# Block-sparse attention into a SoLU layer on one core: the first batch's mask rows in two parts, and four reorderings towards the end of the plan

## The chip, the core and the metric

The kernel runs on one core of a Trainium2 chip. The core has five engines that run side by side and wait for each other by semaphores: TensorE (PE; matmuls and transposes, its weight loads shown apart as PEld), VectorE (DVE), ScalarE (ACT), GpSimd (POOL) and SyncE (SP, which here only issues DMAs). Each engine executes its own instructions in the order in which the program issues them. The metric is the device time of one execution in microseconds (us); less is better.

## The reference

Four batches of eight heads attend over 768 positions with a mask of 32-wide blocks; the result, put together over heads, goes through a layer whose activation is h times softmax(h), a normalisation and a second matmul.

```python
scores = scale * np.matmul(q, k.transpose(0, 1, 3, 2))          # B=4, H=8, S=768, D=64
mask = np.abs(blk_i - blk_j) <= 1                               # blocks of 32
mask |= (blk_i == 0) | (blk_j == 0) | (blk_i == n_blocks - 1) | (blk_j == n_blocks - 1)
...                                                             # and 3 sampled blocks per block row
attn = softmax(np.where(mask, scores, -1e9))
x = np.matmul(attn, v).transpose(0, 2, 1, 3).reshape(B * S, H * D)     # 3072 x 512

h = x @ w_in                                                    # 512 x 1024
solu = h * softmax(h)
ln = (solu - mean(solu)) / np.sqrt(var(solu) + 1e-06) * g_ln
out = ln @ w_out                                                # 1024 x 512
```

## The kernel before

**The attention.** Heads go in pairs (pr = 0 to 3). Queries and keys stand transposed in QT and KT, two of each, used by batches in turn. Partitions 0 to 63 hold the 64 elements of a head; partitions 64 to 87 (`D:KR`) hold mask rows: in KT a selector of the key's block, in QT the mask values of the query for each block. One matmul over 88 partitions thus gives scores with the mask already added (`scores`, L407 to L421). The mask rows are the same for all heads, so those of QT are made once for pair 0 (from `m_ps`, by ScalarE) and copied to the other pairs by `mask_rows` (L663 to L665), which reads `row_q`, the rows of head 0.

The 768 positions of a head are 6 chunks of 128. A pass takes 2 chunks of queries (QW = 256 positions), so a batch takes 3 passes and the kernel 12. A pass has 12 slots: 4 pairs times 3 units, each unit being 2 key chunks. In a slot TensorE makes scores for two slots ahead, ScalarE takes the exponential (`exps`, L423), and TensorE multiplies by the values (`outs`, L431); at the end of a pair VectorE divides by the sums (`normalise`, L451). Score buffers are two, buffers for exponentials three (each holds one pair), and the output of a pair has one PSUM buffer of each of two kinds in the first pass and one afterwards.

**The layer.** x of a pass is transposed by DMA (`x_turn`), except that the first pass and the last chunk of the last pass use TensorE (`x_first`, `x_last`). For each half of a pass: `h_mms` (eight matmuls on TensorE), `e_exp` (exponential with its sum, ScalarE), `solu` (VectorE), `ln_turn` (transposition by DMA), `stats` and `rstd` (VectorE, the root on GpSimd), `o_mms` (eight matmuls with weights whose mean was taken out, `w_cen_sb`), `scaled` and `store`. The layer of one pass runs inside the slots of the next. What is left of pass 10 and pass 11 comes behind the last slot in a list written out by hand (L945 to L983), where the transposition is done by TensorE (`ln_mm`, `ln_out`), the very last output is made in two column halves (`o_half`, `scale_half`), and a flag is worked out that says whether any sum was out of range (`check_r`, `check_e`, `check_sum`, `check_bad`, `check_out`). After everything all engines load the flag, and if it is set the whole is computed again by a slow general path; with these inputs it is not.

**The order.** `at(when, fn, ...)` puts a call on a plan; `emit` sorts the plan by its time in slots and issues it. So a number in `at` is a place in the queue of each engine that the call uses, not a time in microseconds: slot s is `s`, and 144 (`end`) is behind the last. Calls not under `at` are issued at once, before the plan. DMAs for loads, transpositions and most stores go through SP's queue, in the same order.

**Loading the first batch.** Only the first two query chunks of each pair are loaded and transposed at first (`load`, `cast`, `turn_mm`, `turn_out`), which suffices for pass 0; chunks 2 to 5 follow during pass 0 (`turn` at 8.9, 10.9, 14.95 and 16.95). Keys of pair 1 to 3 are transposed with their selector rows and copied out in two parts (`k_out`, L369). VectorE's mask copies of QT[0] stand among these: pair 1 before the plan (L685), pair 2 at 2.0 and pair 3 at 2.9 (L709, L710), each over all 768 positions of two heads, 24 partitions x 1536 elements. GpSimd casts loaded data to bf16 in the same stretch.

**Later batches.** GpSimd casts q and k into `nat`, one DMA per pair transposes both (`turn_dma`), and `shift` (L383) copies the two heads from `pd` into KT or QT on GpSimd, two instructions for each. The last pair's q is shifted in two parts (L806): its first two chunks just before k, and the rest later.

Of the kernel before, what the change touches and what calls it, by code (L numbers as in the profile page):

```python
# [7 lines left out]
FP32 = mybir.dt.float32  # L8
# [200 lines left out]
def kernel(  # L209
# [11 lines left out]
    nc = tc.nc  # L221

    B, H, S, D = q.shape
# [11 lines left out]
    KF = d_ff // 128  # L235
# [6 lines left out]
    PC = 2  # L242
    QW = PC * TQ
    NPB = NCH // PC
    NPASS = B * NPB
    NP = H // 2
# [27 lines left out]
    KT = [fix.tile([128, H * NCH, TQ], BF16, name=f"KT{i}") for i in range(2)]  # L274
    QT = [fix.tile([128, H * NCH, TQ], BF16, name=f"QT{i}") for i in range(2)]
# [14 lines left out]
    def at(when, fn, *args):  # L290
        plan.append((when, len(plan), fn, args))
# [282 lines left out]
    with tc.manual_schedule():  # L574
# [4 lines left out]
                          in_=bass.AP(tensor=_t32, offset=0, ap=[[2 * NR, NB], [1, 2 * NR]]))  # L579
# [59 lines left out]
        for pr in range(1, NP):  # L639
            nc.scalar.activation(  # L640
                out=natural(0, pr, "k")[:, :, :, D:KR].rearrange("p c h r -> p (c h) r"),
                in_=zer[:, 0:NB].rearrange("p (o r) -> p o r", o=1).broadcast_to(
                    [128, NCH * 2, NB]),
# [6 lines left out]
        sel_f = selT.rearrange("p c t -> p (c t)")  # L650
        for i, x0, x1 in ((0, 0, QW), (1, QW, S)):
            nc.tensor.matmul(m_ps[0:KR, i, 0 : x1 - x0], mask_l, sel_f[:, x0:x1],
                             start=True, stop=True)

        def rows(t, h0, h1):
            return t[D:KR].rearrange("p (h c) t -> p h (c t)", c=NCH)[:, h0:h1]

        def spread(x, n):
            return x.rearrange("p (o c) -> p o c", o=1).broadcast_to([NB, n, x.shape[-1]])

        row_q = QT[0][D:KR, 0:NCH, :].rearrange("p c t -> p (c t)")

        def mask_rows(eng, t, h0):  # L663
            eng.tensor_copy(out=rows(t, h0, h0 + 2),
                            in_=spread(sel_f if t in KT else row_q, 2))  # L665

        def selector(pr):
            for base, sg in ((0, 1), (BLK - 1, -1)):
# [11 lines left out]
        for h0, n, i, x0, x1 in ((0, 2, 0, 0, QW), (0, 1, 1, QW, S), (1, 1, 1, QW, S)):  # L680
            nc.scalar.copy(out=rows(QT[0], h0, h0 + n)[:, :, x0:x1],
                           in_=spread(m_ps[D:KR, i, 0 : x1 - x0], n))
        turn_out(0, 0, "q", DVE2, 0, 2)
        turn_out(0, 0, "k", DVE2, 2, NCH)
        mask_rows(nc.vector, QT[0], 2)  # L685
        cast(nc.gpsimd, 0, 1, "k")
        cast(nc.gpsimd, 0, 1, "q", 0, 2)
        scores(0, 2)
# [9 lines left out]
        def turn(when, b, pr, key, pool, c0=0, c1=NCH, engs=DVE2, later=0.02):  # L698
            at(when, turn_mm, b, pr, key, pool, c0, c1)
            at(when + later, turn_out, b, pr, key, engs, c0, c1)  # L700
# [5 lines left out]
        for pr in range(NP):  # L706
            at(0.1, load, nc.sync, q, 0, pr, "q", 2, NCH)

        for pr, w0, w1, w2 in ((2, 1.85, 2.85, 2.0), (3, 4.85, 5.85, 2.9)):  # L709
            at(w2, mask_rows, nc.vector, QT[0], 2 * pr)  # L710
            if pr == 3:
                selector(pr)
            cast(nc.gpsimd, 0, pr, "k")
            cast(nc.gpsimd, 0, pr, "q", 0, 2)
            at(w0, turn_mm, 0, pr, "k", p_h, 0, 2)
            at(w0 + 0.02, k_out, pr, 0, 2)
            turn(w0 + 0.01, 0, pr, "q", p_o, 0, 2)
            at(w1, turn_mm, 0, pr, "k", p_h, 2, NCH)
            at(w1 + 0.03, k_out, pr, 2, NCH)
# [50 lines left out]
        for s in range(n_units):  # L770
            ps, b, j, pr, u = unit(s)
# [25 lines left out]
        for b in range(1, B):  # L797
            loads, casts, turns, shifts, v_loads, v_casts = first if b == 1 else then
            t0 = SLOTS * NPB * (b - 1)
            for (key, pr), t_l, t_c in zip(kq + vs, loads + v_loads, casts + v_casts):  # L800
                at(t0 + t_l, load, nc.sync, srcs[key], b, pr, key)
                at(t0 + t_c, cast, nc.gpsimd, b, pr, key)
            for pr, t_t in enumerate(turns):
                at(t0 + t_t, turn_dma, b, pr)

            at(t0 + shifts[6] - 0.05, shift, b, NP - 1, "q", 0, PC)  # L806
            for (key, pr), t_s in zip(kq, shifts):
                at(t0 + t_s, shift, b, pr, key, PC if (key, pr) == ("q", NP - 1) else 0)


        def layer(ps, i, hs, es, os):
# [14 lines left out]
        LP = NPASS - 1  # L826
# [17 lines left out]
        for i, t0 in ((0, b0), (1, b0 + 4)):  # L844
            for when, n0, n1 in ((3.9, 0, 2), (4.85, 2, 5), (5.86, 5, 8)):
                at(t0 + when, h_mms, ps, i, n0, n1)

            e_at = (6.5, 7.0, 7.05) if i == 0 else (6.85, 6.86, 6.87)
            for when, fn in zip(e_at, (e_exp, solu, ln_turn)):
                at(t0 + when, fn, ps, i)  # L850
        at(b0 + 8.2, stats, ps, 0)
# [2 lines left out]
        def x_last():  # L854
            tp = p_op.tile([128, 1024], BF16, tag="op", name="x_tp")[:, 0 : PC * 128]
            for i in range(PC):
                nc.tensor.matmul(tp[:, i * 128 : (i + 1) * 128],
                                 xb_of[LP][:, KD - 1, i, :], ident,
                                 is_transpose=True, start=(i == 0), stop=(i == PC - 1))
            nc.vector.tensor_copy(  # L860
                out=xT_of[LP][:, (KD - 1) * PC : KD * PC, :],
                in_=tp.rearrange("p (i t) -> p i t", t=128))

# [22 lines left out]

        o2 = {}

        def o_half(half, pool, tag, c0=0, c1=KF):
            if c0:  # L890
                pass
            elif pool is p_sco:
                o2[half] = p_sco.tile([128, 2, HF], FP32, tag=tag, name="oe1a")[:, 0, 0:256]
            else:
                o2[half] = pool.tile([128, d_model], FP32, tag=tag, name="oe1b")[:, 0:256]
            for c in range(c0, c1):
                nc.tensor.matmul(o2[half], lnT_of[LP, 1][:, c, :],
                                 w_cen_sb[:, c, half * 256 : (half + 1) * 256],
                                 start=(c == 0), stop=(c == KF - 1), skip_group_check=True)
# [31 lines left out]
            nc.vector.tensor_scalar(out=bad, in0=n_ok[:, 0:1], scalar1=float(n_r + n_e),  # L931
                                    scalar2=None, op0=ALU.is_lt)

        bad_ps = []

        def check_bad():
            bad_ps.append(p_h.tile([1, 1], FP32, tag="h", name="bad_ps"))
            nc.tensor.matmul(bad_ps[0], bad, ones_c, start=True, stop=True)

        def check_out():  # L940
            nc.vector.tensor_copy(out=bad_i, in_=bad_ps[0])

        end = SLOTS * NPASS
        A, V = nc.scalar, nc.vector
        for n, (fn, *args) in enumerate((  # L945
            (h_end, 0, 2, KD),
            (e_exp, LP, 0),
            (o_mms, LP - 1, 0, 5, 8),
            (scaled, LP - 1, 0, A),
            (store, LP - 1, 0),  # L950
            (stats, LP - 1, 1),
            (rstd, LP - 1, 1),
            (check_r, n_r - 2 * PC, n_r),
            (h_end, 1, 0, KD),
            (solu, LP, 0),
            (stats, LP, 0),
            (e_exp, LP, 1),
            (o_mms, LP - 1, 1, 0, 3, tile_in(p_op, "op", "o_10")),
            (ln_mm, 0),
            (ln_out, 0, A),  # L960
            (o_mms, LP - 1, 1, 3, 8),
            (solu, LP, 1),
            (rstd, LP, 0),
            (stats, LP, 1),
            (o_mms, LP, 0, 0, 2, tile_in(p_sco, "sco", "oe0")),
            (ln_mm, 1),
            (ln_out, 1, A),
            (rstd, LP, 1),
            (check_e,),
            (check_sum,),  # L970
            (o_mms, LP, 0, 2, 8),
            (scaled, LP - 1, 1, A),
            (store, LP - 1, 1),
            (scaled, LP, 0, A),
            (store, LP, 0),
            (o_half, 0, p_sco, "sco"),
            (o_half, 1, p_op, "op", 0, 5),
            (check_bad,),
            (o_half, 1, p_op, "op", 5, KF),
            (scale_half, 0, V, nc.sync),  # L980
            (check_out,),
            (scale_half, 1, A, nc.scalar),
        )):  # L983
            at(end + 0.01 * n, fn, *args)
# [3 lines left out]
        at(end - 1.12, h_end, 0, 0, 2, (1,))  # L988
        at(end - 1.0, x_last)
        at(end - 1.9, check_r, 0, n_r - 2 * PC)  # L990
        at(end - 1.05, o_mms, LP - 1, 0, 0, 5)
        emit()

    work.close()
# [32 lines left out]
```

## Time and profile before

| what | value |
|---|---|
| time, median of 3 executions (lowest, highest) | 210.65 us (210.59, 210.71) |
| the profiled execution | 210.66 us |
| its span in the profile | 208.9 us |
| mean granted TensorE clock | 0.991 |
| engine totals of the page | shown in the prediction |
| DMA moved | 42.02 MB, mean 201 GB/s |

The span runs from the first instruction to the end of the last thing seen; what lies between it and the time is outside the profile. In rows of the timeline the columns are start and duration in us, engine, line of the kernel, operation, output <- inputs, shape, count, and in brackets how long the engine was idle before and for whom it waited; a row can stand for several like instructions in a run. The rows that begin with a stretch A:B give its length, then busy time (and count) of PE, PEld, DVE, ACT and POOL, the granted clock, the DMA share and GB/s. In rows of groups, total busy us and mean ns of one stand behind the bar. Durations of matmuls overlap, since they are pipelined: four matmuls that are shown as 0.60 us let the next one start after 0.44.

### The profile page before, as it was taken

To read this page: it belongs to the slowest core of one execution; us is meant where nothing else is said; L and a number is where in the kernel's file an instruction comes from. 1 tells how busy PE (TensorE), PEld (TensorE's weight loads), DVE (VectorE), ACT (ScalarE), POOL (GpSimd) and SP (SyncE) were. 2 spreads that over 40 slices of the span, in tenths; PEclk is the share of its full clock that TensorE was granted. 3 is DMA by queue.
4 is the path that set the end of the run, shared out by engine and by line. 5 is a ranking of instruction groups with operands and counts; after the bars stand their busy time and mean duration, and the time that the engine had idled before them with its cause. 6 is when DMAs were issued, how large, how long until landed. Compare 5 with 4: busy or idle time off the path is not lost.

```text
span 208.9 us, 5591 instructions
## 1 busy us (share of the span) xinstructions
PE 198.0 (95%) x2204; PEld 137.9 (66%) x2238; DVE 140.3 (67%) x329; ACT 174.6 (84%) x208; POOL 109.1 (52%) x161
## 2 busy tenths in 40 slices
PE   7989999999999999999999999999999999999980
PEld 2669867676676676676666677667667667665450
DVE  5885888987656656666656656656655755768970
ACT  6898989889889889889889889888988988875750
POOL 7989698688686384377196366197450011011120
PEclk9999999999999999999999999999999999999996
DMA  5999999899999899896999899997924915635331
GB/s 159 345 364 220 369 376 275 190 199 307 154 288 277 192 252 264 201 202 169 191 323 198 195 289 236 196 284 90 250 81 89 112 54 81 163 69 84 100 123 37
DMA packets 73906, 42.02 MB, mean 201 GB/s; under 512 B 55828, under 2 KB 69396, under 8 KB 73876
## 3 DMA queue, kind: packets, MB, share of 16 engines
q1 hardware_dynamic: 72932, 40.06, 80.4%
q0 software_dynamic: 528, 1.05, 2.7%
q10 hardware_dynamic: 416, 0.52, 0.8%
q8 instruction: 18, 0.29, 0.6%
q14 instruction: 12, 0.10, 0.2%
HBM read 23.07 MB, written 6.29 MB: 141 GB/s over the span
## 4 chain that ended last, share of the span: by engine, by line
PE 81%; DMA 9%; issue 2%; POOL 2%; ACT 1%; DVE 1%; SPq 1%; POOLq 0%
PE sco L416 28%; PE o L547 17%; PE op L444 16%; PE h L487 16%; DMA st_q<-in_q_dram 3%; DMA w_out_f<-in_moe_w_out_dram 3%; DMA st_k<-in_k_dram 3%; PE he L869 1%; PE oe L547 1%; PE mean_ps L750 1%; POOL VA L327 1%; SPq L318 1%; DVE solu L508 1%; POOL nat L327 1%; ACT e L496 1%
## 5 line engine op out<-in xcount | busy, mean ns | idle before, releaser
L427 ACT ACTIVATE exs<-sco 128x1024 bf16<-128x1024 f32 x144 | 140.6, 1024 | 8.7 <-PE sco L416 6.3
L416 PE MATMUL sco<-QT,KT 88*128 88x256 bf16 x576 | 86.6, 272 | 0.8 <-ACT exs L427 0.5
L416 PEld LDWEIGHTS <-KT 88*128 88x128 bf16 x576 | 54.1, 97 | 32.4 <-issue 5.7
L444 PE MATMUL op<-VA,exs 128*128 128x65 bf16 x1152 | 51.8, 194 | 0.5
L444 PEld LDWEIGHTS <-exs 128*128 128x128 bf16 x1152 | 48.5, 97 | 3.7 <-DVE xb L458 0.3
L487 PE MATMUL h<-w_in_sb,xT 128*128 128x512 bf16 x153 | 48.6, 378 | 0.6
L547 PE MATMUL o<-w_cen_sb,lnT 128*128 128x512 bf16 x166 | 43.2, 379 | 0.5
L540 POOL TENSOR_TENSOR rstd<-vpe,mhalf 128x1 f32<-128x1 f32 x24 | 13.2, 550 | 47.8 <-DVE vpe L538 41.3
L457 DVE RECIPROCAL recip_all<-op 128x4 f32<-128x4 f32 x48 | 8.7, 182 | 41.5 <-PE op L444 41.3
L496 ACT ACTIVATE e<-h 128x1024 bf16<-128x1024 f32 x22 | 22.5, 1024 | 12.3 <-PE h L487 10.8
L522 DVE BATCH_NORM_STATS2 stats<-solu 128x6 f32<-128x512 bf16 x48 | 30.6, 679 | 0.0
L327 POOL COPY KT<-pd 64x768 bf16<-64x768 bf16 x24 | 20.1, 838 | 17.4 <-DMA pd<-nat 15.8
L508 DVE TENSOR_TENSOR solu<-h,e 128x1024 bf16<-128x1024 f32 x22 | 26.7, 1215 | 1.4 <-ACT e L496 1.3
L327 POOL COPY QT<-pd 64x768 bf16<-64x768 bf16 (+2 forms) x30 | 20.8, 694 | 10.8 <-DMA pd<-nat 9.5
L547 PEld LDWEIGHTS <-lnT 128*128 128x128 bf16 x176 | 15.9, 97 | 13.8 <-DMA lnT<-solu 0.2
L558 DVE TENSOR_SCALAR ot<-o,rstd 128x512 f32<-128x512 f32 x20 | 15.0, 750 | 10.8 <-issue 6.9
L458 DVE TENSOR_TENSOR xb<-op,recip_all 128x256 bf16<-128x256 f32 x48 | 20.4, 424 | 1.7
L487 PEld LDWEIGHTS <-xT 128*128 128x128 bf16 x176 | 16.2, 98 | 4.2 <-DMA xT<-xb 0.5
L327 POOL CAST nat<-st_q 128x768 bf16<-128x768 f32 (+2 forms) x19 | 14.0, 736 | 7.8 <-DMA st_q<-in_q_dram 7.7
L327 POOL CAST nat<-st_k 128x768 bf16<-128x768 f32 x15 | 12.7, 850 | 3.3 <-DMA st_k<-in_k_dram 3.0
L327 POOL CAST VA<-st_v 128x768 bf16<-128x768 f32 x16 | 13.4, 842 | 1.9 <-DMA st_v<-in_v_dram 1.3
L740 POOL TENSOR_SCALAR w_out_sb<-w_out_f,g_ln_sb 128x512 bf16<-128x512 f32 x8 | 5.7, 724 | 2.1 <-DMA w_out_f<-in_moe_w_out_dram 2.1
(89 smaller groups left out, 114.7 us busy)
## 6 DMA issues: line engine op xcount, KB each, us to landing
st_v<-in_v_dram SPq DMA_DIRECT2D x16, 384.0 KB, 5.2
out_dram<-ot SPq DMA_DIRECT2D x23, 256.0 KB, 2.8
st_k<-in_k_dram SPq DMA_DIRECT2D x15, 384.0 KB, 5.4
st_q<-in_q_dram SPq DMA_DIRECT2D x12, 384.0 KB, 6.9
w_out_f<-in_moe_w_out_dram SPq DMA_DIRECT2D x4, 512.0 KB, 7.5
st_q<-in_q_dram SPq DMA_DIRECT2D x4, 256.0 KB, 6.9
w_in_sb<-in_moe_w_in_dram POOLq DMA_DIRECT2D x1, 1024.0 KB, 11.5
st_q<-in_q_dram SPq DMA_DIRECT2D x4, 128.0 KB, 4.7
```

What stands on the lines that cost most here:

```text
L327: eng.tensor_copy(out=o, in_=i)
L416: nc.tensor.matmul(sco[:, hh, kk * QW : (kk + 1) * QW], KT[b % 2][0:KR, h * NCH + 2 * u + kk, :], QT[b % 2][0:KR, h * NCH + PC * j : h * N ...
L427: nc.scalar.activation(out=exs_of[ps, pr][:, u].rearrange("p a b c -> p (a b c)"), in_=sco_of.pop(s).rearrange("p a b -> p (a b)"), func=A ...
L444: nc.tensor.matmul(op[:, hh, ic, :], exs[:, u, hh, kk, ic * TQ : (ic + 1) * TQ], VA[b % 2][:, 2 * pr + hh, 2 * u + kk, :], start=(u == 0 a ...
L458: nc.vector.tensor_tensor(out=xb_of[ps][:, pr].rearrange("p c (h d) -> p h c d", h=2), in0=op[:, :, :, 0:D], in1=recip.broadcast_to([TQ, 2 ...
L487: nc.tensor.matmul(h_of[ps, i][:, half, :], xT_of[ps][:, c * PC + i, :], w_in_sb[:, c, half * HF : (half + 1) * HF], start=(c == 0), stop= ...
L496: nc.scalar.activation(out=o, in_=h, func=ACT.Exp, scale=1.0, accum_out=esum_all[:, t : t + 1])
L508: nc.vector.tensor_mul(out=so, in0=h, in1=e)
L522: nc.vector.bn_stats(out=stat_of[ps, i][:, half, :], in_=so[:, half, :])
L540: nc.gpsimd.tensor_tensor(out=rstd_of[ps, i], in0=vpe, in1=mhalf, op=ALU.pow)
L547: nc.tensor.matmul(ops_of[ps, i], lnT_of[ps, i][:, c, :], w_cen_sb[:, c, :], start=(c == 0), stop=(c == KF - 1), skip_group_check=True)
L558: nc.vector.tensor_scalar(out=o, in0=i_, scalar1=r, scalar2=None, op0=ALU.mult)
```

## The change

It has five parts.

- `mask_rows` gets a range of positions. QT[0]'s mask rows of pairs 1, 2 and 3 are copied for the first 256 positions at first (pair 1 before the plan, pair 2 at 2.0, pair 3 at 0.87 instead of 2.9), and for the other 512 positions at 5.9, 7.9 and 8.99.
- The last pair's k of later batches is shifted in two parts like its q: first the first two chunks of k and of q, then the rest of k, and later the rest of q.
- The exponential e of the first half of pass 10's layer comes at 7.01 of the last pass instead of 6.5, which is behind that slot's exponential of scores instead of ahead of it.
- The copy in `x_last` goes to ScalarE, and of the five o matmuls ahead of it two are issued behind its transposes.
- At the end, the sum and the matmul and copy for the flag come behind `scale_half` of the first half instead of among the last matmuls, and `o_half` is in one piece.

```diff
-        def mask_rows(eng, t, h0):
-            eng.tensor_copy(out=rows(t, h0, h0 + 2),
-                            in_=spread(sel_f if t in KT else row_q, 2))
+        def mask_rows(eng, t, h0, x0=0, x1=S):
+            eng.tensor_copy(out=rows(t, h0, h0 + 2)[:, :, x0:x1],
+                            in_=spread((sel_f if t in KT else row_q)[:, x0:x1], 2))
...
-        mask_rows(nc.vector, QT[0], 2)
+        mask_rows(nc.vector, QT[0], 2, 0, QW)
...
-        for pr, w0, w1, w2 in ((2, 1.85, 2.85, 2.0), (3, 4.85, 5.85, 2.9)):
-            at(w2, mask_rows, nc.vector, QT[0], 2 * pr)
+        for pr, when in ((1, 5.9), (2, 7.9), (3, 8.99)):
+            at(when, mask_rows, nc.vector, QT[0], 2 * pr, QW, S)
+        for pr, w0, w1, w2 in ((2, 1.85, 2.85, 2.0), (3, 4.85, 5.85, 0.87)):
+            at(w2, mask_rows, nc.vector, QT[0], 2 * pr, 0, QW)
...
-            at(t0 + shifts[6] - 0.05, shift, b, NP - 1, "q", 0, PC)
             for (key, pr), t_s in zip(kq, shifts):
-                at(t0 + t_s, shift, b, pr, key, PC if (key, pr) == ("q", NP - 1) else 0)
+                if pr == NP - 1:
+                    at(t0 + shifts[6] - 0.1, shift, b, pr, key, 0, PC)
+                at(t0 + t_s, shift, b, pr, key, PC if pr == NP - 1 else 0)
...
-            e_at = (6.5, 7.0, 7.05) if i == 0 else (6.85, 6.86, 6.87)
+            e_at = (7.01, 7.02, 7.05) if i == 0 else (6.85, 6.86, 6.87)
...
-            nc.vector.tensor_copy(
+            nc.scalar.copy(
                 out=xT_of[LP][:, (KD - 1) * PC : KD * PC, :],
...
         def check_bad():
-            bad_ps.append(p_h.tile([1, 1], FP32, tag="h", name="bad_ps"))
-            nc.tensor.matmul(bad_ps[0], bad, ones_c, start=True, stop=True)
-
-        def check_out():
-            nc.vector.tensor_copy(out=bad_i, in_=bad_ps[0])
+            bad_ps = p_h.tile([1, 1], FP32, tag="h", name="bad_ps")
+            nc.tensor.matmul(bad_ps, bad, ones_c, start=True, stop=True)
+            nc.vector.tensor_copy(out=bad_i, in_=bad_ps)
...
             (check_e,),
-            (check_sum,),
...
             (o_half, 0, p_sco, "sco"),
-            (o_half, 1, p_op, "op", 0, 5),
+            (o_half, 1, p_op, "op"),
+            (scale_half, 0, V, nc.sync),
+            (check_sum,),
             (check_bad,),
-            (o_half, 1, p_op, "op", 5, KF),
-            (scale_half, 0, V, nc.sync),
-            (check_out,),
             (scale_half, 1, A, nc.scalar),
...
-        at(end - 1.05, o_mms, LP - 1, 0, 0, 5)
+        at(end - 1.05, o_mms, LP - 1, 0, 0, 3)
+        at(end - 0.95, o_mms, LP - 1, 0, 3, 5)
```

More of the change, by code (lines that the diff above doesn't have):

```diff
@@ L887, with o_half @@
         o2 = {}
[L889 to L892, printed above, removed]
+        def o_half(half, pool, tag):
+            if pool is p_sco:
                 o2[half] = p_sco.tile([128, 2, HF], FP32, tag=tag, name="oe1a")[:, 0, 0:256]
@@ L895, in o_half @@
                 o2[half] = pool.tile([128, d_model], FP32, tag=tag, name="oe1b")[:, 0:256]
-            for c in range(c0, c1):
+            for c in range(KF):
                 nc.tensor.matmul(o2[half], lnT_of[LP, 1][:, c, :],
@@ L932, in check_sum @@
                                     scalar2=None, op0=ALU.is_lt)
-        bad_ps = []
         def check_bad():
-            bad_ps.append(p_h.tile([1, 1], FP32, tag="h", name="bad_ps"))
-            nc.tensor.matmul(bad_ps[0], bad, ones_c, start=True, stop=True)
-        def check_out():
-            nc.vector.tensor_copy(out=bad_i, in_=bad_ps[0])
+            bad_ps = p_h.tile([1, 1], FP32, tag="h", name="bad_ps")
+            nc.tensor.matmul(bad_ps, bad, ones_c, start=True, stop=True)
+            nc.vector.tensor_copy(out=bad_i, in_=bad_ps)
         end = SLOTS * NPASS
```

## The prediction, made before the changed kernel ran

> **What bounds the kernel now.** I read the page's engine totals first, then the table of engines by stretches of time, to see where the load changes.
>
> ```profile
> PE 198.0 (95%) x2204; PEld 137.9 (66%) x2238; DVE 140.3 (67%) x329; ACT 174.6 (84%) x208; POOL 109.1 (52%) x161
> 8.00:16.00 8.00, 6.84 (x74) 5.25 (x73) 6.72 (x14) 7.54 (x8) 6.80 (x12) 1.00 1.08 362
> 96.00:104.00 8.00, 7.89 (x94) 5.50 (x94) 5.05 (x13) 7.09 (x9) 2.66 (x4) 1.00 0.96 146
> 192.00:200.00 8.00, 7.70 (x48) 3.80 (x48) 7.70 (x18) 4.19 (x7) 1.10 (x2) 1.00 0.26 66
> ```
>
> In the middle TensorE is busy 7.89 of 8 us at full granted clock; a microsecond gained ahead of that stretch stays gained, and one gained on another engine inside it is worth nothing. TensorE has air only before 16 us and behind 182 us. The second thing read is the timeline of the start, where ScalarE's exponentials set the pace:
>
> ```profile
> 10.62 0.84 POOL L327 CAST nat<-st_k 128x768 bf16<-128x768 f32 x1
> 9.94 0.69 DVE L371 COPY KT<-tp_k 88x1024 bf16<-88x1024 bf16 x1 [0.49 <-PE tp_k L346]
> 10.81 5.03 ACT L427 ACTIVATE exs<-sco 128x1024 bf16<-128x1024 f32 x5 [0.17 <-PE sco L416]
> 11.10 0.42 DVE L371 COPY KT<-tp_k 88x512 bf16<-88x512 bf16 x1 [0.47 <-PE tp_k L346]
> 12.04 1.04 DVE L664 COPY QT<-QT 24x1536 bf16<-24x1536 bf16 x1
> 12.23 0.60 PE L416 MATMUL sco<-QT,KT 88*128 88x256 bf16 x4
> 13.82 1.11 DVE L664 COPY QT<-QT 24x1536 bf16<-24x1536 bf16 x1
> 14.96 0.42 DVE L371 COPY KT<-tp_k 88x512 bf16<-88x512 bf16 x1
> 15.44 0.61 PE L346 MATMUL tp_k<-ident,nat 128*88 128x128 bf16 x8 [0.66 <-DVE KT L371]
> 16.52 1.02 ACT L427 ACTIVATE exs<-sco 128x1024 bf16<-128x1024 f32 x1 [0.68 <-PE sco L416]
> 17.78 6.74 ACT L427 ACTIVATE exs<-sco 128x1024 bf16<-128x1024 f32 x7 [0.23 <-PE op L444]
> ```
>
> From 11.1 to 15.4 VectorE does one thing after another. The mask copies of pairs 2 and 3 (12.04 and 13.82) push pair 3's key copy to 14.96; TensorE's next transposes wait for it (15.44), the scores behind them are late, and ScalarE idles 0.68 and then 0.23 us: 0.91 us together. From 17.78 it runs without a gap.
>
> **A: mask rows in two parts.** Removed: three copies 24x1536. Added: three 24x512 early and three 24x1024 later, no DMA. Their prices:
>
> ```profile
> 23.47 0.55 DVE L664 COPY KT<-selT 24x1536 bf16<-24x1536 bf16 x1
> L371 DVE COPY KT<-tp_k 88x1024 bf16<-88x1024 bf16 x3 | 2.1, 688 | 0.7 <-PE tp_k L346 0.7
> L371 DVE COPY KT<-tp_k 88x512 bf16<-88x512 bf16 x3 | 1.3, 421 | 0.5 <-PE tp_k L346 0.5
> 13.70 0.82 POOL L327 CAST VA<-st_v 128x768 bf16<-128x768 f32 x1
> 18.95 0.87 DVE L327 COPY QT<-tp_q 64x512 bf16<-64x512 bf16 x2 [0.60 <-PE tp_q L356]
> 19.29 1.46 POOL L664 COPY KT<-selT 24x1536 bf16<-24x1536 bf16 x1
> ```
>
> Two VectorE copies of one kind and half the width differ by 0.267 us, which leaves 0.154 fixed. Of the 0.55 of an undisturbed mask copy 0.40 then go with the width: 0.29 for 24x512 and 0.42 for 24x1024, estimates from these rows. Beside GpSimd the full copy took 1.11: it issued 0.12 after the cast at 13.70 and ended 0.41 after that cast's 14.52, as if it had run its 0.55 from 14.38 on.
>
> The Trainium skill says why (SBUF — State Buffer, Who interferes with whom): a VectorE copy in its two-port mode and a GpSimd instruction exclude each other, and the later one is blocked for the whole of the other's instruction. By that a short copy pays the same wait as a long one, which speaks against cutting one copy in two; the trace agrees (1.11 against 0.55). By the rule A comes to -0.41 below, by its opposite to -0.71.
>
> The first part for pair 3 moves from 2.9 to 0.87 of the plan, behind the 9.94 copy, so it issues near 10.65. If it runs at once it ends at 10.94, in the idle 0.47 ahead of 11.10, and costs nothing. But a cast issued at 10.62; if that is first, the copy runs from 11.32 (the cast's 11.46 less the 0.14 seen above) to 11.61, and the key copy of 11.10 is 0.5 late. Behind it stand eight transposes, then the scores of 12.23, whose 12.83 is just when ScalarE wants them (10.81 + two steps of 1.0). So d = 0.5 is lost there, or 0.
>
> Behind that, with d = 0: pair 2's part ends at 12.04 + 0.29 = 12.33, or 12.8 if blocked as before; pair 2's second key copy follows it, the key copy of pair 3 follows its transposes at about 13.9 instead of 14.96, TensorE's 15.44 becomes 14.4, its next scores wait only for a score buffer (ScalarE's fifth of the run from 10.81, free at about 14.8), and the 0.91 of idle goes. With d = 0.5 the same steps end 0.5 later, still ahead of ScalarE.
>
> The late parts (5.9, 7.9, 8.99) are each up to 0.42 + about 0.5 of waiting in VectorE's queue. The first falls into its pause before the first normalise. The second stands ahead of the copy of pair 0's other queries, and the third ahead of the second normalise, whose output banks the last pair's products need. With d = 0 it issues near 17.4 beside a cast, ends near 18.5, and the query copies (0.87, today 18.95 to 19.82) end at 19.3; 19.82 - 0.91 = 18.91, and some 0.2 behind that are slack, which leaves about 0.2 late. With d = 0.5 all else is later by as much, and this is hidden. So A is -0.91 + 0.2 = -0.71 or -0.91 + 0.5 = -0.41; 10.62 against 10.65 decides nothing where GpSimd's spans are rough, and I take the middle, **-0.56**. Ends: -0.91 (no wait anywhere), and +0.6 (the third late part behind the 1.46 copy of 19.29, about 1.0 on top of -0.41).
>
> **B: the last pair's k in parts.** Today pair 3's k is shifted whole behind a first part of q:
>
> ```profile
> 104.38 0.84 POOL L327 COPY QT<-pd 64x256 bf16<-64x256 bf16 x2 [4.14 <-DMA pd<-nat]
> 105.28 1.71 POOL L327 COPY KT<-pd 64x768 bf16<-64x768 bf16 x2
> 106.61 0.82 PE L416 MATMUL sco<-QT,KT 88*128 88x256 bf16 x4
> 107.99 0.60 PE L416 MATMUL sco<-QT,KT 88*128 88x256 bf16 x4
> ```
>
> The scores at 106.61 took 0.82 instead of 0.60: the second head's keys came at 106.99. The other two batches show no such stretch. After: k's and q's first parts, 4 x 0.4, are through at about 106.0, so the 0.22 goes once; the rest of k, 2 x 0.64 (midway between 0.42 for 256 columns and 0.86 for 768), is there at 107.3, ahead of 107.99. The cut adds 2 x (0.42 + 0.64) - 1.71 = 0.4 us of GpSimd per batch, hidden beside TensorE; uncovered in one batch it would cost those 0.4. **-0.22**, ends -0.22 and +0.2 (the 0.4 less the 0.22).
>
> **C: e behind the exponential.** In the last pass:
>
> ```profile
> 182.09 0.60 PE L416 MATMUL sco<-QT,KT 88*128 88x256 bf16 x4
> 183.63 1.02 ACT L496 ACTIVATE e<-h 128x1024 bf16<-128x1024 f32 x1 [1.41 <-DVE xb L458]
> 183.87 1.68 PE L547 MATMUL o<-w_cen_sb,lnT 128*128 128x512 bf16 x7
> 185.71 0.60 PE L416 MATMUL sco<-QT,KT 88*128 88x256 bf16 x4 [0.17 <-ACT exs L427]
> 170.16 1.67 PE L547 MATMUL o<-w_cen_sb,lnT 128*128 128x512 bf16 x7
> 171.74 0.60 PE L416 MATMUL sco<-QT,KT 88*128 88x256 bf16 x4
> ```
>
> ScalarE idles 1.41 in front of e although scores were complete at 182.69. With the exponential first (182.75 to 183.7), e starts about 0.07 late, and the score buffer is free long before TensorE wants it. From the seven o matmuls to the next scores it takes 1.84 us here and 1.58 a pass earlier, where nothing waits: **-0.26**. Ends: -0.33 and 0 (VectorE, which takes solu from e, becomes late instead).
>
> **D: x's last copy on ScalarE, and two o matmuls behind its transposes.**
>
> ```profile
> 191.66 1.21 DVE L508 TENSOR_TENSOR solu<-h,e 128x1024 bf16<-128x1024 f32 x1
> 192.80 0.28 DVE L860 COPY xT<-x_tp 128x256 bf16<-128x256 bf16 x1
> 193.13 0.82 PE L869 MATMUL he<-w_in_sb,xT 128*128 128x512 bf16 x3 [0.23 <-DVE xT L860]
> 196.05 0.43 PEld L547 LDWEIGHTS <-lnT 128*128 128x128 bf16 x3 [0.22 <-DMA lnT<-solu]
> 202.93 0.47 ACT L906 ACTIVATE ot_last<-oe1b,rstd 128x256 f32<-128x256 f32 x1 [1.14 <-issue]
> ```
>
> The copy waits for VectorE's solu. On ScalarE, idle there, it costs about 0.47 (the same width in the last row), not 0.28, but starts two o matmuls (0.43) earlier, and he begins some 0.3 sooner. That gain meets the wait at 196.05: the transposed lnT hangs on the solu of 191.66, which C alone moves. So **-0.02**; ends -0.3 and 0.
>
> **E: the flag behind the last halves.**
>
> ```profile
> 201.58 0.71 PE L897 MATMUL oe1b<-w_cen_sb,lnTe 128*128 128x256 bf16 x5
> 202.22 0.19 PE L938 MATMUL bad_ps<-ones_c,bad 128*1 128x1 f32 x2
> 202.34 0.50 PE L897 MATMUL oe1b<-w_cen_sb,lnTe 128*128 128x256 bf16 x3
> SPq L1022 <- DMA out_dram<-ot_last: 2.8, 1, 2.8
> ```
>
> Eight oe1b matmuls in a row take 0.71 + 3 x 0.11 = 1.04 from 201.58, so 202.62 instead of 202.84, and ScalarE's scaling and the last store follow: **-0.22**. The flag itself comes 0.5 to 0.7 later against its neighbours (reduce, compare, matmul, copy behind VectorE's scaling), but SyncE waits 2.8 us for the landing of the last store, which covers it; without that cover it would cost up to 0.7.
>
> **Sum.** -0.56 - 0.22 - 0.26 - 0.02 - 0.22 = -1.28 against the profiled execution's 210.66 (span 208.9 and 1.76 around it), which stands 0.01 from the median 210.65: 209.4 us.
>
> **Rivals.**
> 1. The start gives nothing: GpSimd wins at 10.62 and the late parts add 0.4 more. For it speaks that six 24x1536 copies took up to 1.11; against it that the late ones have pauses. Only B to E remain, -0.72: 209.9 us.
> 2. The end gives nothing: C's wait moves to VectorE (solu, scaled, stats and normalise stand in one queue there), and the flag's chain replaces the store's. For it: VectorE is busy 7.70 of 8 us from 192 to 200 in the stretches. Then A and B alone, -0.78: also 209.9 us; both together 210.4.
> 3. The other side: VectorE does not get the port between two GpSimd instructions, but only when GpSimd pauses. GpSimd runs without a pause from 10.62 past 12.7, so the 0.29 us copy ends near 13 and d becomes 1.9; the exponential of 17.78 starts near 18.5 instead, +0.8, and the second late part waits until GpSimd is through with the copy of 19.29 and one more like it, near 22.2, so that the query copies end at 22.2 + 0.4 + 0.9 = 23.5 instead of 19.8: +3.7, or with -0.5 for C to E 213.9 us. It decides from a wait of more than one cast, 0.84 us. Against it: the copy at 13.82 ended 0.41 behind a single cast.
> 4. The reordered instructions find the same order as today on every engine, or the waits found were not what set the end: 210.6 us.
>
> **How the numbers follow.** Forecast 0.65, its own range 208.9 (all the best ends, -1.8) to 209.8. Rivals 1 and 2 together 0.2, rival 3 with its milder forms (the +0.6 end of A, with B at +0.2 and no gain in C) 0.1, rival 4 0.05. The range 208.8 to 210.3 takes in rivals 1 and 2. A change of 0.2% (0.42 us) is about what a measurement of this kernel can tell from none: faster 0.85, same 0.06, slower 0.09.
>
> **What would show it.** A: no wait of 0.68 at the ninth exponential, the gapless run from 17.78 starting at 17.1 to 17.4, and the key copy at 11.10 either unmoved or at 11.6. B: the four scores near 106 take 0.60. C: no idle of 1.41 ahead of e, and 1.58 from o to scores. D: he earlier by 0.6, but the wait for lnT grown to about 0.5. E: eight oe1b matmuls in one piece and 2.5 us or more of waiting for the store. I am wrong if the middle stretches lose TensorE time (below 7.85 of 8), or if the query copies ahead of the second pass come later than the scores want them.

## The result and the profile after

| | median of 6 | lowest to highest |
|---|---|---|
| before | 210.76 us | 210.59 to 211.07 |
| after | 207.67 us | 207.31 to 208.86 |

The ratio is 0.9862, 95% interval 0.9834 to 0.9889: the change saves 3.1 us by the medians where 1.3 were forecast, and 207.67 lies 1.1 below the lower end of the range. The profiled execution of after took 208.32 us, with a span of 206.8.

First the last stretch. The timeline of after, from the last eight matmuls to the last store (columns as above, some rows between left out; the q of ACTq marks the queue's own instructions):

```profile
201.83 1.04 PE L899 MATMUL oe1b<-w_cen_sb,lnTe 128*128 128x256 bf16 x8
202.49 0.37 DVE L932 TENSOR_REDUCE n_ok<-okr 128x1 f32<-128x216 f32 x1
202.96 0.47 ACT L908 ACTIVATE ot_last<-oe1b,rstd 128x256 f32<-128x256 f32 x1 [0.91 <-issue]
203.42 0.15 DVE L939 CAST bad_i<-bad_ps 1x1 int32<-1x1 f32 x1 [0.37 <-PE bad_ps L938]
203.46 0.37 ACTq L563 DMA_DIRECT2D out_dram<-ot_last  x1
```

The eight matmuls take the 1.04 that was forecast, and the flag's copy comes at 203.42 instead of 202.45. The last scaling, though, starts at 202.96, where before had 202.93: in this execution nothing at all was gained up to there. But the span ends 206.8 - 203.46 = 3.3 us behind the issue of the last store, and before it ended 208.9 - 203.44 = 5.5 behind. These 2.1 us are the whole difference of the two spans. The table of waits of SyncE's queue has for after, at the line that ends the kernel:

```profile
SPq L1019 <- PEq L1019: 0.7, 2, 0.5
SPq L1019 <- remote: 0.7, 1, 0.7
```

The wait of 2.8 us for the last store, on which the prediction leant, is gone. Why is seen in the same stretches of time of both kernels (here the last two columns count, DMA share and GB/s). Before:

```profile
204.40:204.80 0.40, 0.00 (x0) 0.00 (x0) 0.00 (x0) 0.00 (x0) 0.00 (x0) 1.00 0.88 289
204.80:205.20 0.40, 0.00 (x0) 0.00 (x0) 0.00 (x0) 0.00 (x0) 0.00 (x0) 0.72 0.18 61
205.20:205.60 0.40, 0.00 (x0) 0.00 (x0) 0.00 (x0) 0.00 (x0) 0.00 (x0) 0.50 0.24 26
205.60:206.00 0.40, 0.00 (x0) 0.00 (x0) 0.00 (x0) 0.00 (x0) 0.00 (x0) 0.50 0.07 10
...
206.80:207.20 0.40, 0.00 (x0) 0.00 (x0) 0.00 (x0) 0.00 (x0) 0.00 (x0) 0.50 0.04 8
```

And after:

```profile
204.40:204.80 0.40, 0.00 (x0) 0.00 (x0) 0.00 (x0) 0.00 (x0) 0.00 (x0) 1.00 0.85 297
204.80:205.20 0.40, 0.00 (x0) 0.00 (x0) 0.00 (x0) 0.00 (x0) 0.00 (x0) 1.00 0.00 0
205.20:205.60 0.40, 0.00 (x0) 0.00 (x0) 0.00 (x0) 0.00 (x0) 0.00 (x0) 1.00 0.42 123
205.60:206.00 0.40, 0.00 (x0) 0.00 (x0) 0.00 (x0) 0.00 (x0) 0.00 (x0) 1.00 0.00 0
```

After, the store moves in one burst that is over by 204.8, there is a pause, and then a second burst. Before, the two run into one, and the transfers drag on until 207.1. The column ahead of these two, the granted clock, differs as well (0.50 before, 1.00 after), but it is not the cause: in the run with part A alone (experiment 6) the transfers drag on in the same way from 204.8 to 206.3, at 8 to 28 GB/s, with a granted clock of 1.00. What the second burst is, the queues tell. Rows of 203 to 208 us, before:

```profile
q10 hardware_dynamic: 144, 0.13, 10.0%
q14 instruction: 4, 0.03, 2.1%
q8 instruction: 1, 0.02, 1.3%
```

and after:

```profile
q10 hardware_dynamic: 144, 0.13, 7.5%
q14 instruction: 4, 0.03, 2.0%
q8 instruction: 1, 0.02, 1.3%
```

q10 is the queue of the last store. Its 144 packets are the same, but before they occupy a third more time. The five packets called instruction are code: one of 16 KB and four of 8 KB, as many as there are engines (that each engine fetches one of them is inferred from their number and times). The single packets of the two traces, in order:

```
             last store issued   store's packets     code packets (start, us each)
before       203.44              204.32 to 207.08    204.61 1.03; 204.80-204.88 0.31-0.44 x3; 205.47 0.55
after        203.46              204.34 to 204.83    205.34 1.02; 205.41-205.51 0.32-0.46 x4
```

Before, 16 of the store's 1 KB packets come one by one from 205.30 on and take 0.05 to 0.70 us each, where 0.05 is usual. The Trainium skill has the two halves of this (Runtime: NRT & Kernel Launch, Instruction fetch mechanics): the engines fetch their code by DMA in blocks, and a taken branch to code that isn't there forces such a fetch before the engine can go on. The trace agrees that code comes as DMA packets, 1.1 to 1.4 us behind the branches (TensorE's branch at 203.48, its 16 KB at 204.61). It does not show the engines waiting for these packets: TensorE's and VectorE's next instructions ran at 203.9 and 204.1, ahead of any of them. They came 0.42 and 0.58 us behind their branches, against 0.28 and 0.24 in the run with a short body (experiment 4), so the engines lost a few tenths at most. It was the store that paid.

The branch is that of the flag: it leaps over the general path. So theory **T1**: the early flag made five engines fetch code into the last store, and the later flag puts the fetch behind it. The rival **T2**: part E is worth its matmuls only (0.22), and the tail differs for some other reason.

### The profile page after: what moved, and what is told of

It reads as the page before. It is cut to its first block, busy times and chain, and to the rows that moved or that the text cites. A ratio compares the mean times of both kernels' runs of the same rounds, so it can differ in the third digit from the quotient of the medians.

```text
span 206.8 us, 5603 instructions
## 1 busy us (share of the span) xinstructions
PE 199.0 (96%) x2204; PEld 138.8 (67%) x2238; DVE 141.1 (68%) x331; ACT 175.2 (85%) x209; POOL 110.2 (53%) x167
## 3 DMA queue, kind: packets, MB, share of 16 engines
q0 software_dynamic: 528, 1.05, 2.7%
## 4 chain that ended last, share of the span: by engine, by line
PE 90%; DMA 4%; DVE 3%; issue 1%; DVEq 0%
PE sco L416 30%; PE op L444 18%; PE o L547 17%; PE h L487 16%; DMA xT<-xb 3%; PE warm_t L403 2%; DMA lnT<-solu 1%; PE tp_k L346 1%; PE oe L547 1%; PE mean_ps L753 1%; PE tp_q L356 1%; PE he L873 1%; DVE KT L371 1%; DVE QT L664 1%; PE ln_tp L883 0%
## 5 line engine op out<-in xcount | busy, mean ns | idle before, releaser
L416 PEld LDWEIGHTS <-KT 88*128 88x128 bf16 x576 | 54.8, 98 | 31.6 <-issue 4.7
L327 POOL COPY KT<-pd 64x768 bf16<-64x768 bf16 (+2 forms) x30 | 21.2, 706 | 23.9 <-DMA pd<-nat 22.8
L538 DVE TENSOR_TENSOR vpe<-es,mv 128x1 f32<-128x1 f32 x24 | 6.7, 278 | 0.9
```

The costliest lines, as they stand in the source:

```text
L327: eng.tensor_copy(out=o, in_=i)
L416: nc.tensor.matmul(sco[:, hh, kk * QW : (kk + 1) * QW], KT[b % 2][0:KR, h * NCH + 2 * u + kk, :], QT[b % 2][0:KR, h * NCH + PC * j : h * N ...
```

## The experiments

Where a run's expectation speaks of before, that is the kernel before run beside it: 210.61 (23 runs) for the first four, 210.68 (17) for the second four, 210.82 (18) for the third.

**1. Part E alone.** The kernel before with only this:

```diff
-            (check_sum,),
...
-            (o_half, 1, p_op, "op", 0, 5),
-            (check_bad,),
-            (o_half, 1, p_op, "op", 5, KF),
+            (o_half, 1, p_op, "op"),
             (scale_half, 0, V, nc.sync),
-            (check_out,),
+            (check_sum,),
+            (check_bad,),
```

> The kernel before with part E alone (flag's reduce, matmul and copy behind the last halves; eight oe1b matmuls in one piece). Before is 210.7 us. T1 (the flag's branch, when it comes early, makes the engines fetch code whose packets get in among those of the last store; later flag, no collision): 208.4 us (-0.2 for the matmuls, -2.1 for the store's landing). T2 (E is worth the matmuls alone, the rest of the gain comes from the other parts): 210.4. By the profile, T1: the wait for the last store's landing on SyncE's queue is gone and the span ends about 3.3 us behind the issue of the last store instead of 5.5; T2: it still ends 5.5 behind.

Measured 208.41, ratio 0.9877 (0.9853 to 0.9902), and no wait for the store. That is T1's value, 2.0 us below T2's.

**2. All but part E.** A, B, C and D on the kernel before, flag in its old place.

> The changed kernel with part E undone (A, B, C and D alone; flag in its place of before). T1: the wait for the last store stays at about 2.8 us and the time is 210.0 (prediction's A to D: 209.6; by the profile of after A is nearly nothing: 210.2). T2: 207.9 to 208.2.

Measured 209.94, ratio 0.9957 (0.9938 to 0.9975). The old wait is back; the row of SyncE's waits:

```profile
SPq L1026 <- DMA out_dram<-ot_last: 2.6, 1, 2.6
```

**3. Only the time of the flag.** Work was added to the kernel before, and nothing else changed:

```diff
         def check_out():
+            for n in range(2):
+                nc.vector.tensor_scalar(out=w_out_f[:, 0, 0:256], in0=o2[0], scalar1=1.0,
+                                        scalar2=None, op0=ALU.mult)
             nc.vector.tensor_copy(out=bad_i, in_=bad_ps[0])
```

> The kernel before with two copies of 128x256 that nothing needs put on VectorE ahead of the flag's last copy, about 0.5 us each: the matmuls keep their order, the flag alone is about 1 us later. T1: 208.6 us, though work was added. T2: 210.7 if the store's landing covers the flag, 211.6 if the flag's chain sets the end.

Measured 208.53, ratio 0.988 (0.9854 to 0.9907). Two useless copies make the kernel 2.1 us faster. It is neither the matmuls' order nor the store that changed, so T2 falls.

**4. A short general path.** If the leap over long code makes the fetch, then a short body behind the branch should heal it with the flag as early as before:

```diff
     with tc.If(n_bad > 0):
-        general_path(tc, q, k, v, sampled_blocks, w_in_sb, w_out_sb, ident, out)
+        nc.vector.memset(ident, 0.0)
```

> The kernel before, flag and all orders as they were, but the general path behind the flag's branch is replaced by one small memset (it leaves out the recomputation, which these inputs don't need). T1 (the branch leaps over long code and makes all five engines fetch code while the last store is under way): without the long leap no code packets of 8 to 16 KB stand beside the store, SyncE's wait for it goes, 208.0 to 208.5 us. T2 (the store is late for another reason, such as the order of the matmuls or of the store itself): 210.6. In between, above 209: the fetch comes whatever the branch leaps over.

Measured 209.08, ratio 0.9927 (0.9904 to 0.995): 0.6 short of T1's value, and in the range given to a fetch that comes whatever the branch leaps over. But no code packet stood near the store, and the timeline and the rows of the branch show a side effect. Timeline:

```profile
202.25 0.47 ACT L906 ACTIVATE ot_last<-oe1b,rstd 128x256 f32<-128x256 f32 x1 [1.14 <-issue]
203.24 0.37 ACTq L563 DMA_DIRECT2D out_dram<-ot_last  x1
```

Instructions of the branch's line:

```profile
L996 ACTq COMPARE_BRANCH  x1: 45/45/45, 203.1 to 203.1; - x1
```

The scaling ended at 202.72, but the store was issued at 203.24, behind ScalarE's branch (203.1); in before it stands ahead of it. A body that doesn't touch the output let the store slip past the branch. The run was made again with a body that writes the same output rows:

```diff
-        general_path(tc, q, k, v, sampled_blocks, w_in_sb, w_out_sb, ident, out)
+        nc.scalar.copy(out=w_out_sb[:, 0, :], in_=w_cen_sb[:, 0, :])
+        nc.scalar.dma_start(out=out[out.shape[0] - 128 : out.shape[0], :],
+                            in_=w_in_sb[:, 0, :].bitcast(FP32))
```

> As the run with the short general path, but its few instructions also write the last rows of the output, so that ScalarE issues the last store ahead of the flag's load and branch, as the kernel before does (there the store stood behind the branch and was issued 0.5 us late). It leaves out the recomputation, which these inputs don't need. T1: 208.6 us (210.7 less the 2.1 that a store without code packets beside it gives); no code packets near the store. T2 (the 0.5 was not the store's place): 209.1 again.

Measured 208.64, ratio 0.9906 (0.9873 to 0.994), as T1 says (the intervals of the two runs overlap; the place of the store is read from the traces). Queues from 203 to 208 us in this run, and SyncE's wait:

```profile
q10 hardware_dynamic: 144, 0.13, 7.5%
q14 instruction: 1, 0.01, 0.6%
```

```profile
SPq L1024 <- DMA out_dram<-ot_last: 1.2, 1, 1.2
```

The one packet of code left comes at 206.6, behind everything. The store takes its 7.5% again, and the flag is as early as before. So it is the leap over the long body. By the records the store lands 1.7 us behind its issue here (203.35 to 205.07), and 4.1 in before (203.44 to 207.54). The two waits are less apart than these, since SyncE comes to its wait at 203.9 here and at 204.7 in before.

**5. How much later is enough.** The changed kernel with `check_sum` one place earlier:

```diff
+            (check_sum,),
             (scale_half, 0, V, nc.sync),
-            (check_sum,),
             (check_bad,),
```

> The changed kernel with the flag's reduce and compare ahead of VectorE's scaling instead of behind it: the flag comes some 0.7 us earlier than in the changed kernel and 0.2 later than before. The code packets should then start near 204.8, just behind the store's last packets (204.8). T1 with no overlap left: the end hangs on the flag's own chain, 0.6 us earlier than the changed kernel (207.7): 207.1. T1 with overlap: 208.5 to 209.7. T2 (the fetch doesn't matter): 207.7.

Measured 207.66, ratio 0.985 (0.983 to 0.9871): no meeting of the packets, but no 0.6 gained either. T2 gives 207.7 as well, so this run does not tell the theories apart; it shows how early the flag may come. The runs by the distance of the flag's copy from the last store's issue, both read from the timelines:

| runs | flag's copy ahead of the store's issue | SyncE waits for the store |
|---|---|---|
| before; part E undone; A alone; C and D; B alone | 0.98 to 0.99 us | 2.5 to 2.8 us |
| delayed flag; this run; shift with it (below) | 0.40 to 0.43 us | no wait |
| after; E alone; shift; all but A | 0.04 us | no wait |
| short general path, in order | 0.99 us | 1.2 us |
| short general path, store behind the branch | 1.48 us | 1.7 us |

With the long body the border lies between 0.43 and 0.98. Beyond it hardly more is to be had: in this run the span ends 206.1 - 202.9 = 3.2 us behind the store's issue, where after has 3.3. The store landed at 204.61, and SyncE's step that needs it ran at 204.74, so the two are nearly level.

**6. Part A alone.**

> The kernel before with part A alone (mask rows of the first batch's q in two parts). The prediction: 210.1 (-0.56). Rival, that the start gives nothing because the late parts and the blocked copy take back what the early one gives: 210.7; by the single profile of after, in which TensorE was slow until 9.6 us, it could be +0.3: 211.0. All the idle gone and no wait: 209.8.

Measured 210.12, ratio 0.9972 (0.9951 to 0.9992), -0.49. The size is as predicted, the way is not. In the first pass the exponentials gained what was hoped for; at 45 us most of it was gone. This table shows by how much an exponential's start differs from that of before, read from the single records of the traces (exponentials are counted from 0, 12 to a pass):

```
exponential         0      9     18     33     36     78     84
A alone         -0.55  -1.43  -1.32  -1.33  -0.19  -0.19  -0.41
```

The 0.55 at number 0 is none of A's: the runs with the delayed flag and with C and D, which have no A, stand 0.54 ahead there. From number 0 to 9 the gain is 0.88. The timeline of this run at the place of the loss:

```profile
41.28 0.16 DVE L538 TENSOR_TENSOR vpe<-es,mv 128x1 f32<-128x1 f32 x1
42.20 1.92 POOL L327 COPY KT<-pd 64x768 bf16<-64x768 bf16 x2
44.20 0.57 POOL L540 TENSOR_TENSOR rstd<-vpe,mhalf 128x1 f32<-128x1 f32 x1
44.81 0.75 DVE L558 TENSOR_SCALAR ot<-o,rstd 128x512 f32<-128x512 f32 x1 [1.56 <-POOL rstd L540]
47.66 1.21 DVE L508 TENSOR_TENSOR solu<-h,e 128x1024 bf16<-128x1024 f32 x1
```

The root's input was there at 41.44, but GpSimd was at a shift until 44.1 and made the root at 44.20, the same time as in before, whatever the start had gained. VectorE's scaling waited 1.56 us for it, and the next `solu`, for which TensorE's matmuls h were waiting, came as late as before.

**7. The shift behind the root.** So the changed kernel with one number of the plan changed (list `first`, second batch):

```diff
-            [21.3, 21.4, 26.0, 27.3, 30.1, 30.15, 38.2, 39.0],
+            [21.3, 21.4, 27.25, 27.3, 30.1, 30.15, 38.2, 39.0],
```

> The changed kernel with one more move: GpSimd's shift of pair 1's k of the second batch goes from 26.0 to 27.25 of the plan, behind the first root of the normalisation instead of ahead of it. T-A1 (in the run with part A alone, the exponentials were 0.85 us ahead of before by 46 us, and 0.55 of it was lost there since VectorE's first output scaling waited 1.56 us for that root on GpSimd, behind the shift): 207.2 us, half a microsecond below the changed kernel's 207.7. T-A2 (what was lost there is lost at the next meeting with GpSimd's or the loads' own pace): 207.7.

Measured 206.64, ratio to before 0.9817 (0.9784 to 0.9851): a microsecond below the changed kernel, twice what was expected, and the lowest median of all runs here. In its timeline the scaling has no wait:

```profile
42.19 0.87 POOL L540 TENSOR_TENSOR rstd<-vpe,mhalf 128x1 f32<-128x1 f32 x1 [0.69 <-DVE vpe L538]
43.02 1.70 POOL L327 COPY KT<-pd 64x768 bf16<-64x768 bf16 x2
43.76 0.74 DVE L558 TENSOR_SCALAR ot<-o,rstd 128x512 f32<-128x512 f32 x1
```

Its exponentials are 0.73 ahead at number 18 and 0.74 at number 36: nothing is given back. Whether the shift does that by itself, the same kernel without part A tells.

> The changed kernel with part A undone and the shift behind GpSimd's root. If the shift only keeps what A gains in the first pass, then without A it is worth no more than the 0.22 us that VectorE's scaling waited for the root before: 208.0 (210.7 - 2.2 for E - 0.22 for B - 0.3 for C and D, less 0 to 0.2). If the shift is worth a microsecond by itself: 207.0.

Measured 207.80, ratio 0.9856 (0.9827 to 0.9884). E, B, C and D as measured alone give 207.8 from this before (210.82 - 2.20 - 0.45 - 0.37), so the shift alone is worth nothing that the times show; A on top of it is worth about a microsecond (206.64 against 207.80). The records agree: between number 35 and 36 the exponentials of the three runs with the shift moved stay where they are against before (0.01 us), and those of the others fall back by 0.05 to 1.15. Both moves together, the shift and the flag in the middle:

> The changed kernel with both moves together: the shift behind GpSimd's root, and the flag's reduce ahead of VectorE's scaling. With the code packets just behind the store's, and the end hanging on the flag's chain (bad_i 0.4 us ahead of the last store's issue instead of level with it): 206.2 us, 0.45 below the 206.64 of the shift alone. If the end hangs on the store's landing by then: 206.6. If the packets meet: 207.5 or more.

Measured 206.73, ratio 0.9803 (0.9774 to 0.9832): no better than the shift alone, which fits the expectation's 206.6, the store's own landing as the floor at the end. Its profiled execution was its slowest (208.12), and shows one thing that the prediction feared for A:

```profile
19.82 1.46 POOL L664 COPY KT<-selT 24x1536 bf16<-24x1536 bf16 x1
20.07 1.49 DVE L664 COPY QT<-QT 24x1024 bf16<-24x1024 bf16 x1
21.34 1.55 POOL L664 COPY QT<-QT 24x1536 bf16<-24x1536 bf16 x1
```

The third late part, 0.42 when alone, stood beside GpSimd's copy and took 1.49; the exponentials, 0.10 us behind those of before at number 13, were 0.84 behind from number 16 on. It depends on which of the two comes first by a few tenths: in the run with A alone the same copy took 0.55, issued at 18.55.

**8. C and D; B.**

> The kernel before with parts C and D alone (e of pass 10 behind the exponential; x's last copy on ScalarE). The prediction: 210.4 (-0.26 - 0.02). Rival, that the wait for lnT takes both: 210.65. By the profile of after, where the last exponentials came 0.37 earlier and the wait for lnT rose from 0.22 to 0.61: 210.5. The flag and the store keep their places, so the landing of the last store is as late as before.

Measured 210.31, ratio 0.9981 (0.9964 to 0.9997), -0.37.

> The kernel before with part B alone. The prediction: 210.45 (-0.22); in the profile the scores near 106 take 0.60 and the exponentials behind them come 0.22 earlier against those ahead. Rival: the stretch is a matter of a few tenths in the arrival of the transposed data (it was absent in the run with part A alone, without B), so B is worth 0 to 0.2 by the run: 210.6.

Measured 210.37, ratio 0.9987 (0.9965 to 1.0008), -0.45 and not told apart from 0 by the times. In its records the exponentials step from -0.06 to -0.28 between number 78 and 84, just the 0.22. The same step stands in the table above for the run with A alone, which has no B; there the scores in question:

```profile
106.42 0.60 PE L416 MATMUL sco<-QT,KT 88*128 88x256 bf16 x4
```

Where the work runs a few tenths ahead of before, the stretch of 0.82 isn't there to be saved, so B's 0.22 and A's overlap.

## Why the prediction was wrong

**E failed, in its second sentence.** "The flag itself comes 0.5 to 0.7 later ..., but SyncE waits 2.8 us for the landing of the last store, which covers it." The flag came 0.97 later (203.42 against 202.45) and cost nothing, so far well. But the 2.8 us were taken as a property of the store, as if nothing in the change touched them, and the term had no end below -0.22. They were made by the early flag: with its code packets out of the way the store lands 1.7 us behind its issue instead of 4.1; the wait is 1.2 us where the flag is as early as before, and none where it is late. The term of -0.22 should have been -2.2 (run 1: 210.61 - 208.41), of which the matmuls are 0.2 and the tail 2.0. None of the rivals had it: the only one that touches the flag, rival 2, asked what the later flag could cost, and not what the early one was costing. The sign for E, "2.5 us or more of waiting for the store", is the one that failed outright.

The row that could have told was there in the trace of before. For the stores of line L563 from 200 us on whose landing it shows, it gives:

```profile
DMA to landing us min/median/max: 1.9/2.0/2.1
```

The wait of 2.8 us began behind all other work (SyncE's own steps went on to 204.7) and reached to 207.5, 4.1 us behind the last store's issue: twice what a store of this line takes to land.

**A: right in size by luck (-0.56 against -0.49), wrong in its account.** The 0.68 ahead of the ninth exponential is gone, in the run with A alone from -0.55 to -1.43, 0.88 us of the 0.91. The undisturbed costs were right too: in after the first part for pair 3 takes 0.28 (estimate 0.29), a late part 0.42 (0.42). In after's execution, the start:

```profile
11.60 0.28 DVE L664 COPY QT<-QT 24x512 bf16<-24x512 bf16 x1
11.75 6.10 ACT L427 ACTIVATE exs<-sco 128x1024 bf16<-128x1024 f32 x6 [0.30 <-PE sco L416]
12.33 1.60 POOL L327 CAST VA<-st_v 128x768 bf16<-128x768 f32 x2
12.98 1.10 DVE L664 COPY QT<-QT 24x512 bf16<-24x512 bf16 x1
18.09 6.74 ACT L427 ACTIVATE exs<-sco 128x1024 bf16<-128x1024 f32 x7 [0.24 <-PE op L444]
20.34 0.42 DVE L664 COPY QT<-QT 24x1024 bf16<-24x1024 bf16 x1
```

A short copy beside GpSimd pays a wait, but not always the one reckoned: the copy at 12.98 took 1.10 for 0.28 and ended 0.15 behind the second of the two casts shown above it (13.93), so it was not let in between them, which is what rival 3 says. In the run with the shift moved, a copy of that size at 10.54 took 0.79 and ended 0.14 behind a single cast (10.35 to 11.19), although the next cast followed at once. So the traces have both, as far as GpSimd's rough spans tell. The sum took 0.2 to 0.5 off the 0.91 for such waits; the run with A alone had lost 0.03 of it at number 9 and 0.14 at number 18. What the working took for granted is its sentence that a microsecond gained ahead of the middle stays gained: TensorE is busy there, but GpSimd's root at 44.20 sits in the path, and there most of the gain was lost until the shift was moved. What that trace keeps at its last exponential, -0.44, is the -0.19 from 36 on and the step of 0.22 near 106 us (experiment 8), and neither is in A's working.

One thing of after's own execution is no part of A: a middle stretch lost TensorE time (7.48 of 8 us, 7.95 in before), which was named as a sign of being wrong.

```profile
128.00:136.00 8.00, 7.48 (x86) 5.25 (x87) 5.64 (x13) 6.70 (x9) 3.82 (x5) 1.00 1.27 196
```

```profile
134.64 0.11 PEld L487 LDWEIGHTS <-xT 128*128 128x128 bf16 x2 [0.49 <-DMA xT<-xb]
```

A transposition by DMA was late, and the exponentials there fell back by 0.55 us. None of the traces of the twelve runs has such a step there (at most 0.05), so it is laid to that execution; why the transposition was late is open.

**B: -0.22 as worked out** where the data come as late as in before, else nothing.

**C and D: the parts right, the sum a little small** (-0.28 against -0.37). After:

```profile
183.41 1.02 ACT L427 ACTIVATE exs<-sco 128x1024 bf16<-128x1024 f32 x1 [0.51 <-PE sco L416]
184.33 1.02 ACT L496 ACTIVATE e<-h 128x1024 bf16<-128x1024 f32 x1
184.55 1.68 PE L547 MATMUL o<-w_cen_sb,lnT 128*128 128x512 bf16 x7
186.06 0.60 PE L416 MATMUL sco<-QT,KT 88*128 88x256 bf16 x4
192.65 0.37 ACT L864 COPY xT<-x_tp 128x256 bf16<-128x256 bf16 x1 [1.00 <-PE x_tp L861]
196.40 0.33 PEld L547 LDWEIGHTS <-lnT 128*128 128x128 bf16 x3 [0.61 <-DMA lnT<-solu]
```

The idle time ahead of e is gone, o to scores takes 1.51 (forecast 1.58), and the exponentials step by -0.37 between number 138 and 141 in all seven kernels that have C. D's copy took 0.37 instead of 0.47, and its gain met the wait for lnT, 0.61 instead of 0.22, as forecast (0.5).

**The sum.** The parts measured alone are -2.20 (E), -0.49 (A), -0.45 (B) and -0.37 (C, D), -3.5 together; the change gave -3.1 and A to D together -0.67 of -1.31. E alone and A to D together, -2.20 and -0.67, make -2.9. B's and A's overlap is 0.22 of what is missing; the rest is within the intervals. The range has a slip of its own: the best ends of A to D and E's -0.22 add up to -1.98, not -1.8, so to 208.7, still a microsecond above what was measured.

## What to carry to other kernels

A long wait at the end of a kernel is not a cover but a finding: look which packets move in it before leaning on it. In this kernel a branch over long code was followed, 1.1 to 1.4 us later, by code packets that delayed the last store; let the store be out before them, here by having the flag ready at most 0.4 us ahead of the store's issue. And a gain ahead of a busy stretch is kept only if every engine in the path gets earlier, down to a root of 128 numbers queued on GpSimd behind a copy of 1.9 us.

## What was not expected of the hardware

- Beside five code packets of 8 and 16 KB the end of a store of 128 KB took 2.3 us longer (last packet 207.08 against 204.83 us, issued within 0.02 us of each other). The code's own packets were through at 206.02; why the store's still came one by one until 207.08 the runs don't tell. The Trainium skill (DMA: Bandwidth & Descriptors, Queues, rings and completion order) says that a DMA engine takes the queues in turn, a packet each; that fits the pause from 204.80 to 205.30, in which no packet of the store starts while the 16 KB packet (204.61 to 205.64) and the others move, not the slow ones afterwards.
- TensorE reached its full pace at different times from run to run while the granted clock read 1.00 throughout. Four transposes at 9.07 us of after took 0.63, four at 8.04 of before 0.39; the row of the eight first scores, which can hold waiting between them, took 1.92 and 1.05:

```profile
7.36 1.92 PE L416 MATMUL sco<-QT,KT 88*128 88x256 bf16 x8
9.07 0.63 PE L346 MATMUL tp_k<-ident,nat 128*88 128x128 bf16 x4
```

This put the first exponentials of after's profiled execution 0.68 to 0.99 us behind those of before, though no instruction of TensorE ahead of them was changed, and the profiled execution with both moves showed it too (eight scores in 1.92). Together with the late transposition (0.55) it is why that profile shows no gain up to the last store, and why one profile alone would have judged A wrongly.
